# Zero-padding the 64-row key tail to 128 rows and transposing the query tail as whole 128x128 blocks in a fused attention and expert kernel

## The chip, the cores and the metric

The program runs on one core of one Trainium2 chip. The metric is the device time of one execution in microseconds (us); lower is better. A kernel's time is the median of its runs.

## The reference, cut to what matters

Three layers follow each other: a linear attention, a dense layer with an ELU, and four weighted experts. The change touches the attention alone, which works on `q`, `k`, `v` of shape (4 batches, 8 heads, 576 positions, 64):

```python
def phi(x):
    proj = np.einsum('bhsd,df->bhsf', x, w_phi)          # 64 -> 128 features
    proj = proj - np.max(np.abs(proj), axis=-1, keepdims=True)
    return np.concatenate([np.exp(proj), np.exp(-proj)], axis=-1)
q_p, k_p = phi(q), phi(k)
kv  = np.einsum('bhsf,bhsd->bhfd', k_p, v)
z   = np.sum(k_p, axis=2)
num = np.einsum('bhsf,bhfd->bhsd', q_p, kv)
den = np.einsum('bhsf,bhf->bhs', q_p, z)[..., None] + 1e-06
return num / den
```

The result, as 2304 rows of 512, goes through `elu(x @ w_in) @ w_out` with 2048 hidden features and then through four experts with 1024 hidden features each.

## The kernel before, in words

**The attention** goes by pairs of heads: `pair(i)` (L169 to L335) is a generator for one pair, and there are 16 pairs. A sequence of 576 positions is four blocks of 128 and a tail of 64. The host has laid out the last 64 positions of k and of q side by side, so that one matmul (L215) projects both tails at once into a tile whose rows 0 to 63 are the key tail and rows 64 to 127 the query tail; `guard` (L199 to L203) subtracts the row maximum and leaves it in `md`.

From there the two halves go different ways. The key half is exponentiated with both signs into `kpm` (L224, by `kexp`, L205 to L207), a tile of 64 rows. For each of two heads h and two signs c, `kv(h, c)` (L234 to L237) sums k_p^T v in PSUM: four matmuls of 128 rows from `kp` (L236), then one of 64 rows from `kpm` (L237), with `v` in a tile `vt` whose unset columns hold 1.0 so that z comes out beside kv. A float32 matmul is two instructions, so one pair has 32 of L236 and 8 of L237, and "one tail" below means one such L237 matmul of two instructions; there are 4 tails in a pair and 64 in all. The query blocks are transposed on the matmul engine (`tpose`, L239 to L244; the instruction is on L243, four 128x128 blocks in one call), and the query tail by two transposes of rows 64 to 127 (L281), each giving 64 columns. `qexp` (L252 to L262) exponentiates the transposed blocks out of PSUM.

Pairs 0 to 6 (`wide`, i < `NF32`) hold their operands as float32; the other nine split them into a high and a low float32r part on ScalarE and GpSimd (L181, L182, L261, L266).

**The order of the work.** The program is written out in Python, as generators that are advanced in turn: `attention()` starts a new pair every `ATT_LAG` = 5 steps; `weight_stream()` loads the 64-bit weights of the dense layer and converts each piece in steps (`convert64`, L100 to L121: loads on SP at L102, ScalarE at L108, L114, L119, VectorE at L110 to L113, GpSimd at L116, L118, L121) through `CVB` = 3 buffers into a ring of 16 weight tiles. The main loop (L744 on) mixes them with units of the dense layer (`Elu`, matmuls at L524 to L526 and L553 to L555), which goes through all 2304 rows twice, for the first and the second half of the hidden features. The weights of the second half go into the ring as the first half's last row tiles release it. A scheduler that places instructions by its own estimate of their times then fixes the order on each engine. After the attention come the rest of the dense layer and the expert stage, which the change does not touch.

**What sets up the tiles.** `ident`, the two `vt` tiles and `wbl` are made on GpSimd at the start (L157 to L164, of which the `vt` memsets on L160). `kpm` is allocated anew for each pair, from one buffer.

Of the kernel before, what the change touches and what calls it, by code (L numbers as in the profile page):

```python
# [8 lines left out]
F32 = mybir.dt.float32  # L9
# [8 lines left out]
B, H, S, D, FEAT = 4, 8, 576, 64, 128  # L18
NT, DM, DFF, E, F2 = 2304, 512, 2048, 4, 1024
P = 128  # L20
# [42 lines left out]
def attn_elu_moe_kernel(ctx: ExitStack, tc: tile.TileContext, kq_in, vv, w_phi, w_in, w_out, probs, w1, w2, out):  # L63
    nc = tc.nc
    V, A, G, PE, SP = nc.vector, nc.scalar, nc.gpsimd, nc.tensor, nc.sync
# [5 lines left out]
    def pool(name, bufs=1, stack=ctx, **kw):  # L71
        return stack.enter_context(tc.tile_pool(name=name, bufs=bufs, reuse_waits="tile", **kw))
# [53 lines left out]
    a1 = pool("a1", stack=att)  # L126
    wbd = a1.tile([P, 2, FEAT], F32, name="wbd")
    ident = a1.tile([P, P], F32, name="ident")
# [4 lines left out]
    def load(i):  # L133
        b, p = divmod(i, NP)
        kq = ld.tile([P, 2 * S], F32, tag="kq", name="kq")
        SP.dma_start(kq[:, :640], kq_in[b, p, :, :640])
        if i == 0:
            SP.dma_start(wbd, w_phi)
        SP.dma_start(kq[:, 640:], kq_in[b, p, :, 640:])
        v = vt[i % 2]  # L140
        SP.dma_start(v[:, 0:4, 0:D], vv[b, p, :, 0:4, :])
        SP.dma_start(v[:, 4:8, D:P], vv[b, p, :, 4:8, :])
        SP.dma_start(v[0:D, 8, 0:D], vv[b, p, 0:D, 8, :])
        SP.dma_start(v[0:D, 9, D:P], vv[b, p, D:P, 8, :])
        return kq, v

    def bank(shape=(P, 512)):
        return psum.tile(list(shape), F32, tag="bank", name="bank")
# [9 lines left out]
    for i in range(2):  # L158
        t = a1.tile([P, 10, P], F32, name=f"vt{i}")
        G.memset(t, 1.0)  # L160
        vt.append(t)
    loaded = {0: load(0)}
    A.activation(wbh, wbd, ACTF.Copy)
    G.tensor_tensor(out=wbl, in0=wbd, in1=f32(wbh), op=ALU.subtract)  # L164

    def blocks(t, n):
        return t[:, :n * P].rearrange("p (n f) -> p n f", f=P)

    def pair(i):  # L169
        b, p = divmod(i, NP)  # L170
        kq, v = loaded.pop(i)
# [33 lines left out]
        def kexp(d0, d1, src):  # L205
            A.activation(d0, src, ACTF.Exp)
            A.activation(d1, src, ACTF.Exp, scale=-1.0)  # L207

        kp = [a1.tile([P, 4, 2, P], F32, tag=f"kp{j}", name=f"kp{j}") for j in range(2)]
        kpm = a1.tile([D, 2, 2, P], F32, tag="kpm", name="kpm")  # L210
        md = a1.tile([P, 2, P], F32, tag="md", name="md")
        qd = [a1.tile([P, 4, P], F32, tag=f"qd{j}", name=f"qd{j}") for j in range(2)]
        kh = halves(kt)
# [7 lines left out]
        guard(kp[1][:, :, 1], proj(kh, 1), 4)  # L221
        qh = halves(qt)
        yield
        kexp(kpm[:, :, 0], kpm[:, :, 1], md[:D])  # L224
        kexp(kp[1][:, :, 0], kp[1][:, :, 1], kp[1][:, :, 1])
        guard(qd[0], proj(qh, 0), 4)
        if i + 1 < B * NP:
# [4 lines left out]
        pk = bank((P, 4, P))  # L232

        def kv(h, c):  # L234
            for t in range(4):
                PE.matmul(pk[:, 2 * h + c], kp[t // 2][:, t % 2 * 2 + h, c], v[:, 4 * h + t], start=(t == 0), stop=False)  # L236
            PE.matmul(pk[:, 2 * h + c], kpm[:, h, c], v[:D, 8 + h], start=False, stop=True)  # L237

        def tpose(j):  # L239
            pt = bank()  # L240
# [9 lines left out]
            el = a1.tile([P, 2, 2, S], F32R, tag="el", name="el")  # L250

        def qexp(ps, c0, n):  # L252
            src = ps[:, :2 * n].rearrange("p (h s) -> p h s", h=2)
            if wide:
                for c, sc in ((0, 1.0), (1, -1.0)):
                    A.activation(ew[:, :, c, c0:c0 + n], src, ACTF.Exp, scale=sc)
                return None
            ef = a1.tile([P, 2, 2, n], F32, tag=f"ef{n}", name="ef")
            for dst in (ef, eh[:, :, :, c0:c0 + n]):
                for c, sc in ((0, 1.0), (1, -1.0)):  # L260
                    A.activation(dst[:, :, c], src, ACTF.Exp, scale=sc)  # L261
            return ef  # L262
# [7 lines left out]
        else:  # L270
            kvh = a1.tile([P, 4, P], F32R, tag="kvh", name="kvh")
            kvl = a1.tile([P, 4, P], F32R, tag="kvl", name="kvl")
        ef0 = qexp(tpose(0), 0, 256)
        kv(0, 0)
        kv(0, 1)
        yield
        split(ef0, 0, 256)
        ef1 = qexp(tpose(1), 256, 256)
        pt = bank()
        for h in range(2):  # L280
            PE.transpose(pt[:, h * D:(h + 1) * D], md[D:P, h], ident[D:P, D:P])  # L281
        efm = qexp(pt, 512, D)
        kv(1, 0)
        kv(1, 1)
        A.activation(kvw if wide else kvh, pk, ACTF.Copy)
# [53 lines left out]
    def attention():  # L339
        live = []  # L340
        nxt = 0
        step = 0
        while nxt < B * NP or live:
            if nxt < B * NP and step % ATT_LAG == 0:
                live.append(pair(nxt))
                nxt += 1
            for g in list(live):
                if next(g, True):
                    live.remove(g)
                    done[0] += 1  # L350
                else:
                    yield
            step += 1
# [528 lines left out]
```

## Time and profile before

| what | value |
|---|---|
| runs | 1439.26 us median of 3 (1438.32 to 1442.92) |
| the profiled execution's own time | 1437.72 us |
| its span, first to last instruction | 1435.9 us |
| TensorE (PE) busy, matmuls | 1406.3 us, 98% of the span |
| VectorE (DVE), ScalarE (ACT), GpSimd (POOL) busy | 703.2, 621.7, 446.3 us |
| chain of work that ended last | PE 81%, DVE 9%, DMA 4%, issue 2%, ACT 2%, POOL 2% |

In the table and the rows below, PE is the engine's matmuls and PEld its weight loads, which overlap them. L237 is line 237 of the kernel. A busy share of PE says little by itself, because matmuls are pipelined and the profile models their ends; the chain says better how far apart they come. In the chain, the length of a piece is how far it moves the end of the work on. An engine's idle time is followed in brackets by what ended it.

### The profile page before, as it was taken

The page shows a single profiled execution, that of the slowest core. Times are in us where ns is not written, and L with a number is a line of the kernel's source. Part 1 is how long each engine was busy: PE and PEld are TensorE (multiplying, and loading weights), DVE is VectorE, ACT ScalarE, POOL GpSimd, SP SyncE. Part 2 cuts the span into 40 slices and gives each one's busy share as a digit, 9 for nine tenths or more (in the row PEclk, how much of TensorE's full clock was granted, in tenths as well). Part 3 has the DMA queues.
Part 4 walks back from the last instruction along what each step waited for, and adds up shares of the span by engine and source line. Part 5 has one row for each costly group of instructions (what it writes and reads, how often), then busy time and mean ns, then how long its engine had stood idle before and what let it go on. Part 6 is the DMA issues. An engine that isn't in the chain of part 4 may idle for free.

```text
span 1435.9 us, 22308 instructions
## 1 busy us (share of the span) xinstructions
PE 1406.3 (98%) x8688; PEld 1295.8 (90%) x8688; DVE 703.2 (49%) x1150; ACT 621.7 (43%) x1348; POOL 446.3 (31%) x498
## 2 busy tenths in 40 slices
PE   7999999999999999999999999999999999999998
PEld 6788999999998999999989989898888989899897
DVE  7999746556489735333434333233432335233332
ACT  6777666576566544334333443122332214222121
POOL 4567654443388712115111341001330004300000
PEclk9999999999999999999999999999999999999999
DMA  4433222111233335313243323524144352433421
GB/s 149 132 117 113 95 66 65 46 56 46 89 97 124 119 118 214 109 43 118 91 152 121 118 67 121 208 89 166 47 147 154 101 204 69 139 110 132 159 83 66
DMA packets 93625, 160.22 MB, mean 112 GB/s; under 512 B 28496, under 2 KB 39888, under 8 KB 93520
## 3 DMA queue, kind: packets, MB, share of 16 engines
q1 hardware_dynamic: 93520, 158.80, 33.4%
q8 instruction: 68, 1.11, 0.3%
q14 instruction: 37, 0.30, 0.1%
HBM read 109.22 MB, written 49.55 MB: 111 GB/s over the span
## 4 chain that ended last, share of the span: by engine, by line
PE 81%; DVE 9%; DMA 4%; issue 2%; ACT 2%; POOL 2%; SPq 0%; DVEq 0%; POOLq 0%; ACTq 0%
PE bank L700 9%; PE bank L701 8%; PE bank L702 8%; PE bank L641 8%; PE bank L643 8%; PE bank L642 8%; PE bank L236 4%; PE bank L524 4%; PE bank L526 3%; PE bank L554 3%; PE bank L553 3%; PE bank L525 3%; PE bank L555 3%; PE bank L315 3%; DVE top L112 2%
## 5 line engine op out<-in xcount | busy, mean ns | idle before, releaser
L700 PE MATMUL bank<-w,h 128*128 128x512 f32 x576 | 224.6, 392 | 3.9 <-ACT h L652 3.9
L641 PE MATMUL bank<-xv,w 128*128 128x384 f32 x672 | 224.2, 339 | 2.4 <-ACT cm L647 2.4
L642 PE MATMUL bank<-xv,w 128*128 128x384 f32 x672 | 226.6, 337 | 0.0
L701 PE MATMUL bank<-w,h 128*128 128x512 f32 x576 | 225.5, 392 | 0.0
L643 PE MATMUL bank<-xv,w 128*128 128x384 f32 x672 | 223.7, 338 | 0.0
L702 PE MATMUL bank<-w,h 128*128 128x512 f32 x576 | 198.3, 391 | 0.7 <-DVE h L653 0.7
L461 POOL TENSOR_TENSOR w<-wst,w 128x256 fp32r<-128x256 f32 x80 | 62.6, 800 | 341.3 <-ACT w L460 337.2
L554 PE MATMUL bank<-gl,w 128*128 128x256 f32 x576 | 162.1, 286 | 4.1 <-DVE gl L537 4.0
L555 PE MATMUL bank<-gh,w 128*128 128x256 f32 x576 | 160.1, 283 | 0.0
L553 PE MATMUL bank<-gh,w 128*128 128x256 f32 x576 | 155.8, 287 | 2.4 <-ACT gh L536 2.3
L641 PEld LDWEIGHTS bank<-xv,w 128*128 128x128 f32 x672 | 126.6, 188 | 10.3 <-ACT cm L647 3.3
L653 DVE SCALAR_TENSOR_TENSOR h<-bank,h 128x384 fp32r<-128x384 f32 x144 | 77.3, 554 | 115.5 <-ACT h L652 115.5
L652 ACT ACTIVATE h<-bank 128x384 fp32r<-128x384 f32 x144 | 66.8, 490 | 151.3 <-PE bank L643 92.0
L700 PEld LDWEIGHTS bank<-w,h 128*128 128x128 f32 x576 | 108.6, 188 | 25.0 <-ACT h L652 5.3
L642 PEld LDWEIGHTS bank<-xv,w 128*128 128x128 f32 x672 | 126.8, 189 | 4.4
L701 PEld LDWEIGHTS bank<-w,h 128*128 128x128 f32 x576 | 108.6, 189 | 20.6
L643 PEld LDWEIGHTS bank<-xv,w 128*128 128x128 f32 x672 | 126.3, 188 | 0.0
L702 PEld LDWEIGHTS bank<-w,h 128*128 128x128 f32 x576 | 107.3, 188 | 20.0 <-DVE h L653 1.6
L554 PEld LDWEIGHTS bank<-gl,w 128*128 128x128 f32 x576 | 110.1, 191 | 6.7 <-DVE gl L537 5.9
L553 PEld LDWEIGHTS bank<-gh,w 128*128 128x128 f32 x576 | 106.0, 191 | 5.3 <-ACT gh L536 4.4
L555 PEld LDWEIGHTS bank<-gh,w 128*128 128x128 f32 x576 | 110.0, 191 | 0.3
L647 ACT ACTIVATE cmab<-bank 128x384 f32<-128x384 f32 x48 | 23.6, 492 | 178.5 <-PE bank L643 178.5
(118 smaller groups left out, 3005.2 us busy)
## 6 DMA issues: line engine op xcount, KB each, us to landing
xv<-xvd SPq DMA_DIRECT2D x42, 768.0 KB, 4.4
wst<-in_w SPq DMA_DIRECT2D x64, 256.0 KB, 2.8
xvd<-xv SPq DMA_DIRECT2D x21, 768.0 KB, 4.4
yscr<-y SPq DMA_DIRECT2D x54, 256.0 KB, 2.1
y<-yscr SPq DMA_DIRECT2D x54, 256.0 KB, 2.9
w<-in_w_in SPq DMA_DIRECT2D x32, 256.0 KB, 2.8
w<-in_w_out SPq DMA_DIRECT2D x32, 256.0 KB, 2.7
kq<-in_kq SPq DMA_DIRECT2D x16, 320.0 KB, 3.0
```

Source lines behind the costliest of these rows:

```text
L461: on[WL[v % len(WL)]].tensor_tensor(out=lo, in0=x, in1=f32(hi), op=ALU.subtract)
L553: PE.matmul(o, w[:, 0, c], self.gh[:, j], start=start, stop=False)
L554: PE.matmul(o, w[:, 0, c], self.gl[:, j], start=False, stop=False)
L555: PE.matmul(o, w[:, 1, c], self.gh[:, j], start=False, stop=stop)
L641: PE.matmul(o, hi[:, c], x[:, 0, kc], start=not more and kc == 0, stop=False, skip_group_check=more)
L642: PE.matmul(o, hi[:, c], x[:, 1, kc], start=False, stop=False, skip_group_check=more)
L643: PE.matmul(o, lo[:, c], x[:, 0, kc], start=False, stop=kc == 1, skip_group_check=more)
L652: A.activation(h[:, 0], c, ACTF.Relu)
L653: V.scalar_tensor_tensor(out=h[:, 1], in0=c, scalar=0.0, in1=f32(h[:, 0]), op0=ALU.max, op1=ALU.subtract)
L700: PE.matmul(self.acc, h[:, 0, c], w[:, 0], start=f == 0, stop=False)
L701: PE.matmul(self.acc, h[:, 0, c], w[:, 1], start=False, stop=False)
L702: PE.matmul(self.acc, h[:, 1, c], w[:, 0], start=False, stop=f == 2 * NQ - 1)
```

## The change

`kpm` becomes one tile of 128 rows for all pairs, allocated once and set to zero on GpSimd before the first load. The exponentials write its rows 0 to 63 as before; rows 64 to 127 stay zero. The tail matmul reads all 128 rows of `kpm` and of `vt` (whose rows 64 to 127 hold 1.0 there, and count as zero in the product). The query tail's transposes take both 128x128 blocks of `md` whole, against the whole identity, and `qexp` reads columns 64 to 127 of each transposed block.

```diff
@@ set-up, after vt
+    kpm = a1.tile([P, 2, 2, P], F32, name="kpm")
+    G.memset(kpm, 0.0)
@@ pair(i)
-        kpm = a1.tile([D, 2, 2, P], F32, tag="kpm", name="kpm")
@@
-        kexp(kpm[:, :, 0], kpm[:, :, 1], md[:D])
+        kexp(kpm[:D, :, 0], kpm[:D, :, 1], md[:D])
@@ kv(h, c)
-            PE.matmul(pk[:, 2 * h + c], kpm[:, h, c], v[:D, 8 + h], start=False, stop=True)
+            PE.matmul(pk[:, 2 * h + c], kpm[:, h, c], v[:, 8 + h], start=False, stop=True)
@@ qexp(ps, c0, n)
-            src = ps[:, :2 * n].rearrange("p (h s) -> p h s", h=2)
+            src = ps[:, :512].rearrange("p (h s) -> p h s", h=2)[:, :, :n] if n > P else blocks(ps, 2)[:, :, P - n:]
@@ the query tail
-            PE.transpose(pt[:, h * D:(h + 1) * D], md[D:P, h], ident[D:P, D:P])
+            PE.transpose(pt[:, h * P:(h + 1) * P], md[:, h], ident)
```

## Rows read from the trace of the kernel before

**Rows 1.** Span and granted TensorE clock of the core.

```profile
core 0: 1435.9 us, clock 0.997
```

**Rows 2.** Busy us of each engine (instructions) by stretch; then granted clock, DMA share, GB/s.

```profile
20.00:100.00 80.00, 77.68 (x446) 64.72 (x445) 75.43 (x143) 60.65 (x155) 47.80 (x67) 1.00 0.40 121
100.00:140.00 40.00, 39.80 (x269) 35.30 (x268) 37.46 (x69) 26.91 (x65) 28.56 (x38) 1.00 0.39 120
140.00:365.00 225.00, 225.00 (x1738) 212.84 (x1738) 134.37 (x194) 145.74 (x329) 111.23 (x120) 1.00 0.19 60
...
400.00:480.00 80.00, 73.92 (x574) 69.75 (x574) 73.32 (x130) 51.39 (x120) 65.96 (x82) 1.00 0.31 103
```

**Rows 3.** The chain's shares by line in 140 to 365 us.

```profile
by line: PE bank L236 16.5%; PE bank L315 13.0%; PE bank L553 8.0%; PE bank L555 7.9%; PE bank L554 7.9%; PE bank L524 7.8%; PE bank L526 7.4%; PE bank L525 7.2%; PE bank L237 6.6%; PE bank L194 4.1%; PE bank L196 3.8%; PE bank L195 3.7%; P
```

**Rows 4.** The chain's shares by line in 20 to 100 us, then in 400 to 480 us.

```profile
by line: DVE rc L324 11.3%; PE bank L236 8.8%; DVE top L112 6.8%; DVE mx L202 6.2%; DMA w<-in_w_out 5.7%; PE bank L315 4.9%; DVE xf L327 4.0%; issue 3.9%; PE bank L237 3.6%; DVE kp L203 3.0%; ACT kp L206 2.9%; DVE qd L203 2.8%; ACT kp L207 
...
by line: DVE top L112 21.7%; DVE top L111 13.0%; issue 10.7%; DVE top L110 10.4%; DVE gl L537 9.4%; DVE pw L113 9.0%; DVE g L535 8.4%; DMA wst<-in_w 3.9%; DMA w<-in_w_in 3.6%; POOL low L116 3.2%; POOL w L121 2.7%; POOL top L118 2.5%; ACT gh
```

**Rows 5.** Single lines: xcount, ns min/median/max, first and last start; rows*columns of the array.

```profile
L236 PE MATMUL bank<-vt,kp x512: 270/275/377, 14.1 to 359.9; 128*128 128x128 f32 x171
...
L237 PE MATMUL bank<-vt,kpm x128: 272/322/373, 15.1 to 360.3; 64*128 64x128 f32 x128
...
L281 PE MATMUL bank<-ident,md x32: 221/247/275, 19.5 to 359.5; 64*128 64x64 f32 x32
```

**Rows 6.** Pieces of the chain around one pair's tails: start us, length us, what.

```profile
329.15 0.44 PE bank L243 x4
329.58 0.89 PE bank L236 x8
330.48 0.41 PE bank L237 x2
330.89 1.09 PE bank L236 x8
331.98 0.42 PE bank L237 x2
332.40 0.32 PE bank L555
332.94 0.12 PE bank L555
...
335.35 0.27 PE bank L281 x2
335.62 1.09 PE bank L236 x8
```

**Rows 7.** L237 alone by stretch: length, PE busy us (instructions), PEld busy (instructions), clock, DMA.

```profile
0.00:20.00 20.00, 1.46 (x6) 0.88 (x6) 1.00 0.61 183
20.00:100.00 80.00, 8.25 (x34) 5.00 (x34) 1.00 0.40 121
100.00:140.00 40.00, 3.88 (x16) 2.35 (x16) 1.00 0.39 120
140.00:365.00 225.00, 17.47 (x72) 10.59 (x72) 1.00 0.19 60
```

**Rows 8.** Timeline of POOL at the start: start us, us, what [idle before].

```profile
0.87 2.27 POOL L160 MEMSET vt<- 128x1280 f32 x2
...
12.56 0.78 POOL L116 TENSOR_TENSOR low<-low,pw 128x256 f32<-128x256 f32 x1 [7.34 <-DVE pw L113]
```

**Rows 9.** Timeline of ACT near 388 us: the first conversions of the second half's weights.

```profile
388.57 0.72 ACT L119 ACTIVATE w<-top 128x256 fp32r<-128x256 f32 x2 [0.40 <-PE bank L526]
```

**Rows 10.** Pieces of the chain near 65 us: where the scheduler put L215.

```profile
64.91 0.42 PE bank L236 x2
65.32 0.43 PE bank L215 x2
65.76 0.67 PE bank L236 x6
```

**Rows 11.** A piece of the chain in the early stretch.

```profile
22.52 4.53 DMA w<-in_w_out
```

## The prediction

> **What bounds the kernel now.** First the core's span and clock [rows 1]: the clock is at its full level almost throughout, so no time is to be won or lost there. Then the busy time by stretch [rows 2], because the change lies wholly before 365 us and the question is what ends last there. From 140 to 365 us PE is busy for all of 225 us while VectorE works for 134 and no other engine for over 146. From 20 to 100 us PE (77.7 of 80) and VectorE (75.4) are both nearly full, and so from 100 to 140 us. From 400 to 480 us VectorE is again near its end (73.3 of 80).
>
> A busy PE may be waiting inside, so the chain decides. In 140 to 365 us all its large shares are PE's own lines [rows 3]: what makes PE's instruction stream shorter there makes the kernel shorter. In 20 to 100 us the two largest groups on VectorE's side, the reciprocal L324 and the conversion L112, alternate with PE and ACT, and L237 has a small share; in 400 to 480 us the chain is VectorE's conversions [rows 4]. So a gain on PE should arrive nearly whole in the long stretch and only in part in the early one.
>
> **What a tail costs now.** The edited matmul and transposes are the only three forms to compare [rows 5]: L236 uses 128 rows of the array, L237 and L281 use 64, and 128 L237 instructions make 64 tails. The page's durations are modelled, so I price them by how far they move the chain [rows 6]. Eight L236 after 128-row work take 0.89 us, 0.111 each. The two L237 of a tail take 0.41 where two L236 would take 0.22: 0.19 more. The eight L236 behind the tail take 1.09 instead of 0.89: 0.20 more. That second part is not peculiar to L236, for L555 behind another tail takes 0.32 where its next takes 0.12. A tail thus costs 0.39 us over two 128-row instructions in its place. For the query tail, the two L281 take 0.27 where two of the four L243 (0.44 for four, 0.11 each) take 0.22, and the eight L236 behind take 1.09, not 0.89: 0.05 + 0.20 = 0.25 us for each pair.
>
> **What the change makes of it.** A padded tail has the form of L236, and whole-block transposes have the form of L243. Bounds for the new tail's instruction are 0.111 us (L236) and 0.205 us (L237 as it stands); I take 0.111, since shape, type and operand memory are then those of L236. For the transposes the bounds are 0.11 (L243) and 0.135 (L281 now); I take 0.11. Saved on PE: 64 x 0.39 = 25.0 us and 16 x 0.25 = 4.0 us, 29.0 us in all, or 0.45 us for each tail with its quarter of a pair of transposes.
>
> By stretch [rows 7], two instructions a tail: 3 tails before 20 us, 17 in 20 to 100, 8 in 100 to 140, 36 in 140 to 365. At 0.45 each that is 1.4, 7.7, 3.6 and 16.2 us of PE time.
>
> How much of each arrives:
> - 140 to 365 us: PE is the chain, so nearly all. Waits of a few tenths may come up between PE and ACT or GpSimd, whose slack is 79 and 114 us of 225. Bounds 12 and 16.2; I take 16.0.
> - 100 to 140 us: the chain can shorten by at most VectorE's idle time, 40 - 37.46 = 2.5 us, if VectorE's work stays put. Bounds 0.5 and 3.6 (where VectorE's backlog is worked off later, behind PE's); I take 2.0.
> - 20 to 100 us: VectorE's idle time is 80 - 75.43 = 4.6 us; the PE gain is 7.7. Bounds 0.5 and 7.7; with two nearly full engines in turn on the chain I take about half of VectorE's room, 2.5.
> - Before 20 us there are many waits besides; bounds 0 and 1.4; I take 0.5.
>
> Sum: 16.0 + 2.0 + 2.5 + 0.5 = 21.0 us.
>
> **What else is added or moved.** The memset of 512 columns goes to GpSimd once. Two memsets of 1280 columns took 2.27 us [rows 8], so 512 cost some 0.45 us, an estimate from that row; bounds 0.1 and 1.1. GpSimd has 7.34 us idle before its first conversion step in the same rows, which hides it; only `wbl` is queued behind it, and the narrow pairs need that first, over 100 us later. Without the cover the price would be those 0.45 us once. The first tail gains a wait for that memset, which ends near 3.6 us, while the first tail starts at 15.1 [rows 5]; behind it on PE would be the whole stream, but it is over by 11 us. The exponentials write as many elements as before and `qexp` reads as many; its 64-column runs now lie 128 apart, which I put at nothing, between -1 and +1 us over 16 pairs since PE and not ACT ends the stretch. The next pair's exponentials wait for this pair's tails as before, since `kpm` had one buffer. No DMA is added or moved, and no queue passed.
>
> **Does the gain last beyond 365 us?** The VectorE-bound stretch from 400 us would swallow it if its work were waiting for something else than PE. But the first piece of the second half's weights, L119, was released by PE's L526 [rows 9]: the ring slot comes free when the first half's last matmul on it ends. The stretch should begin earlier by what PE gained, unchanged in length, and all that follows with it.
>
> The profiled execution took 1437.72 us, 1.8 over its span; less 21.0 that is 1416.7. The median of the runs shown is 1.5 us higher, so the forecast against it is **1418 us**.
>
> **A rule that speaks against it.** In the rows a 64-row instruction is dearer than a 128-row one of equal columns [rows 5, 6]. The Trainium skill, page "TensorE: Matmul & The Clock Gate", section "LDWEIGHTS (loading the stationary operand)", says that a weight load takes its time from the number of columns and that the count of rows doesn't matter, and its closing table says that one matmul of 32 rows takes the same time as one of 128. By that rule padding buys nothing on the tail, the first rival below; the trace disagrees with it by 0.39 us a tail.
>
> **The rivals.**
> 1. *The surcharge isn't that of 64 rows.* L237 also closes the sum in PSUM, and reads its own tile; if one of these costs the 0.39 us, the padded tail keeps it. Against it: L281 closes no sum and the work behind it pays the same 0.20 us. What is left then is at most the transposes' 4.0 us on PE, 9 of 16 pairs in the long stretch: 0 to 3 us, so about 1437 us. Chance 0.07.
> 2. *All of it arrives.* VectorE only filled its time because it waited its turn among PE's results, and works its conversions off later, where it has 91 us of room: 29 us, 1410 us. Against it stand VectorE's 94% in 20 to 140 us. Chance 0.08.
> 3. *Freed time turns into waits.* The narrow pairs' splits on ACT and GpSimd come late for a faster PE, in the long stretch too, and a third to two thirds of the 21 us are lost: 5 to 13 us, about 1430 us. Against it: in that stretch neither engine is busy for two thirds of the time. Chance 0.10.
> 4. *Slower: conversions slip.* The scheduler places work by its own times, and it does mix pairs: L215 of the next pair stands inside one kv sum [rows 10]. With other tails and transposes it may put VectorE's conversion steps behind the reciprocals in the early stretch, so that a weight buffer is refilled late. One such refill on the chain cost 4.53 us [rows 11]. It takes five of them to eat 21 us; six give 27 - 21 = +6, about 1445 us. Nothing in the profile asks for that many. Chance 0.07, of which 0.01 ends within the bound of no change.
>
> **How the numbers follow.** The forecast, a gain of 13 to 25 us, has 0.68. A measurement can tell some 0.3% from no change, 4.3 us: the forecast and rivals 2 and 3 are faster (0.68 + 0.08 + 0.10 = 0.86), rival 1 and the mild end of rival 4 are the same (0.08), the rest of rival 4 slower (0.06). The range takes the forecast's 1414 to 1426, most of rival 2 down to 1411 and the near part of rival 3 up to 1428; beyond lie the rest of rivals 2 and 3 and all of 1 and 4.
>
> **What would show it.** L237 and L281 stand in the new trace as 128*128 forms; two tail instructions take 0.22 us of the chain, and eight L236 behind a tail 0.89 again. The attention's last L236 starts near 339 us instead of 359.9; the stretch in which VectorE is full stays as long and begins some 21 us sooner; VectorE's share in 20 to 100 us goes above 94%. Wrong would be: pieces of 0.41 us at 128 rows (rival 1); PE waits for ACT or POOL in the long stretch (3); a weight load on the early chain several times over, with PE idle behind it (4).

## The result, and the profile after

The changed kernel takes **1423.53 us** (median of 4 runs, 1422.43 to 1424.97) against 1438.79 us for the kernel before in the same comparison (median of 4, 1437.66 to 1442.92). The ratio is 0.9889, 95% interval 0.9867 to 0.9911: 15.3 us, or 1.1%, faster. The profiled execution took 1424.05 us with a span of 1422.3 us. The forecast was 1418 us within 1411 to 1428, so the time lies inside the range, 5.5 us on the slow side.

First the price, the part that a reader can check piece by piece against [rows 6]. The changed lines in the new trace (L237 is the old L236, L238 the old L237, L244 the old L243, L282 the old L281), forms first and then the chain around one pair (start us, length us):

```profile
L238 PE MATMUL bank<-vt,kpm x128: 273/275/275, 15.0 to 344.1; 128*128 128x128 f32 x128
```

```profile
321.36 0.44 PE bank L244 x4
321.80 0.22 PE bank L282 x2
322.01 0.89 PE bank L237 x8
322.91 0.22 PE bank L238 x2
323.13 0.89 PE bank L237 x8
324.03 0.22 PE bank L238 x2
324.25 0.12 PE bank L196
```

Two tail instructions take 0.22 us instead of 0.41, the eight instructions behind them 0.89 instead of 1.09, two transposes 0.22 instead of 0.27, with 0.89 behind them. The prices came out as written, to the last digit that the view shows.

Next, the stretches, to hold against [rows 2] (busy us of PE, PEld, DVE, ACT and POOL with counts; then clock, DMA share, GB/s):

```profile
20.00:100.00 80.00, 70.05 (x437) 61.31 (x436) 77.23 (x146) 60.33 (x155) 49.11 (x69) 1.00 0.41 124
100.00:140.00 40.00, 39.03 (x291) 36.72 (x292) 33.45 (x71) 27.29 (x68) 28.62 (x39) 1.00 0.40 125
140.00:342.00 202.00, 200.32 (x1657) 198.51 (x1656) 132.38 (x186) 139.43 (x312) 102.43 (x110) 1.00 0.21 65
...
400.00:480.00 80.00, 73.41 (x572) 69.39 (x571) 69.26 (x120) 50.84 (x118) 65.54 (x79) 1.00 0.34 111
```

From 20 to 100 us PE has fallen from 77.7 to 70.1 busy us, while VectorE has gone up to 77.2 of 80. PE's new idle time there is a wait for VectorE: the transposes L244 (the old L243) wait for the query blocks that VectorE makes (engine, line, what it waited for: us in all, times, longest; before, then after):

```profile
PE bank L243 <- DVE qd L203: 1.8, 2, 1.3
...
PE bank L244 <- DVE qd L205: 6.9, 5, 2.0
```

and in the chain of that stretch, which PE shared before [rows 4], VectorE's lines now lead (those shown add up to 65%, before to 34%):

```profile
by line: DVE rc L325 15.2%; DVE mx L204 12.1%; DVE top L112 7.5%; DVE xf L328 7.1%; issue 6.8%; DVE top L110 6.6%; DVE qd L205 5.2%; DVE kp L205 4.0%; DVE top L111 3.7%; DMA w<-in_w_in 3.4%; DVE pw L113 3.2%; PE bank L194 3.2%; PE bank L316
```

Where the gain arises and where it is given back can be read off milestones: the start of the last tail instruction of a pair, of the first second-half weight (L119, its 33rd), and of the first matmul of the expert stage (us from the span's start, from the two traces). A milestone compares like with like only where PE has started as many matmul instructions before it in both, so their number stands beside it:

| milestone | before | after | gain | instructions before it |
|---|---|---|---|---|
| last tail of pair 0 | 21.09 | 19.56 | 1.5 | 69, 69 |
| last tail of pair 4 | 84.22 | 82.90 | 1.3 | 408, 408 |
| last tail of pair 6 | 138.91 | 135.79 | 3.1 | 765, 765 |
| last tail of pair 8 | 188.48 | 186.95 | 1.5 | 1139, 1157 |
| last tail of pair 9 | 212.07 | 206.62 | 5.5 | 1321, 1321 |
| last tail of pair 15 | 360.30 | 344.13 | 16.2 | 2471, 2471 |
| first second-half weight written | 388.57 | 374.86 | 13.7 | 2704, 2726 |
| first matmul of the expert stage | 665.05 | 650.65 | 14.4 | 4896, 4896 |
| span | 1435.9 | 1422.3 | 13.6 | 8688, 8688 |

Pair 8's 1.5 is not a loss of that size, because in the changed kernel the scheduler has put 18 more matmuls of the dense layer ahead of that tail, some 2.2 us at 0.12 us each (PE's count in the first bracket; before, then after, up to just short of the tail):

```profile
0.00:188.47 188.47, 178.53 (x1139) 155.53 (x1140) 158.28 (x293) 131.34 (x318) 118.62 (x156) 1.00 0.38 118
0.00:186.94 186.94, 166.89 (x1157) 153.04 (x1158) 156.34 (x293) 131.95 (x321) 118.45 (x157) 1.00 0.39 120
```

Some 29 us of PE time were removed, 1.81 a pair; 16.2 are left when the attention's last tail starts. From pair 9 to pair 15 the gain grows by 10.7, all but 0.2 of what these six pairs free. Pairs 7 to 9 bring 2.3 of 5.4, and pairs 0 to 6 bring 3.1 of 12.7. Then 2.5 are lost again before the second half's weights start. The experiments ask why. (The two profiled executions lie 13.7 us apart, the medians 15.3; runs of one kernel differ by up to 5 us here, so the milestones account for the traces and not for the last 2 us.)

### The profile page after: what moved, and what is told of

It reads as the page before. It is cut to its first block, busy times and chain, and to the rows that moved or that the text cites. A ratio compares the mean times of both kernels' runs of the same rounds, so it can differ in the third digit from the quotient of the medians.

```text
span 1422.3 us, 22325 instructions
## 1 busy us (share of the span) xinstructions
PE 1380.5 (97%) x8688; PEld 1286.9 (90%) x8688; DVE 698.2 (49%) x1150; ACT 619.9 (44%) x1348; POOL 446.7 (31%) x499
## 4 chain that ended last, share of the span: by engine, by line
PE 74%; DVE 11%; DMA 5%; POOL 4%; issue 3%; ACT 3%; SPq 0%; DVEq 0%; POOLq 0%; ACTq 0%
PE bank L701 8%; PE bank L702 8%; PE bank L703 8%; PE bank L642 8%; PE bank L643 7%; PE bank L644 7%; PE bank L555 3%; PE bank L556 3%; PE bank L554 3%; PE bank L527 3%; PE bank L525 3%; PE bank L526 3%; PE bank L237 2%; PE bank L316 2%; DMA wst<-in_w 2%
## 5 line engine op out<-in xcount | busy, mean ns | idle before, releaser
L556 PE MATMUL bank<-gh,w 128*128 128x256 f32 x576 | 160.9, 284 | 0.0
L703 PEld LDWEIGHTS bank<-w,h 128*128 128x128 f32 x576 | 107.3, 188 | 20.0 <-DVE h L654 1.6
L556 PEld LDWEIGHTS bank<-gh,w 128*128 128x128 f32 x576 | 110.1, 191 | 0.2
```

The costliest lines, as they stand in the source:

```text
L556: PE.matmul(o, w[:, 1, c], self.gh[:, j], start=False, stop=stop)
L703: PE.matmul(self.acc, h[:, 1, c], w[:, 0], start=False, stop=f == 2 * NQ - 1)
```

## The experiments

The theory: a 64-row instruction among 128-row ones costs PE the surcharge of [rows 6]; PE sets the end behind 140 us, and VectorE does before. The rivals: that the surcharge belongs to something else than the 64 rows; and that part of the gain is lost in every pair alike. Each set of runs had its own runs of the kernel before (medians of 1439.5 to 1441.0 us), so the ratios are compared, not the medians.

**1. The two edits apart.** Padded tails alone (e1), whole transposes alone (e2):

```diff
  e1: the changed kernel, with
-            PE.transpose(pt[:, h * P:(h + 1) * P], md[:, h], ident)
+            PE.transpose(pt[:, h * D:(h + 1) * D], md[D:P, h], ident[D:P, D:P])
  (and qexp's source as before);  e2: the kernel before, with the reverse
```

> Only the key tail is padded; the query tail's transposes stay at 64 rows. Theory (each 64-row tail costs 0.39 us of PE more than a 128-row one, each pair's transposes 0.25): tail pieces of 0.22 us and 0.89 us behind them, L282 still 0.27 and 1.09; 25 of the 29 us of PE go, so 25/29 of the whole change's 15 us arrive: 12 to 14 us below the kernel before. Rival (the whole-block transposes bring most of it): under 5 us.

> Only the query tail's transposes are whole blocks; the key tail stays at 64 rows. Theory: L281 takes 0.22 us for two and the eight matmuls behind it 0.89; 4 of 29 us of PE go, 2.2 of them after 140 us: 1.5 to 3 us below the kernel before. Rival (64-column transposes cost no more than others in the stream): within 1 us of the kernel before.

The tails alone: 1425.15 us, ratio 0.9895 (0.9881 to 0.9910), as much as the whole change within the intervals. The transposes alone: 1440.27 us, 0.9999 (0.9988 to 1.0010): nothing, where 1.5 to 3 us were expected, a miss. In e2's trace pair 15's last tail starts 1.0 us sooner than before (359.26), but the first second-half weight 1.9 us later (390.43). What lies between shows in the number of matmul instructions that PE has started up to that weight, x in the first bracket (stretch from 0 to the start of L119's 33rd; the kernel before, the changed one, e1, e2):

```profile
0.00:388.57 388.57, 378.63 (x2704) 346.68 (x2705) 269.87 (x448) 255.58 (x589) 202.13 (x244) 1.00 0.29 89
```

```profile
0.00:374.86 374.86, 354.81 (x2726) 340.54 (x2727) 269.39 (x449) 255.66 (x591) 204.30 (x246) 1.00 0.30 93
```

```profile
0.00:374.08 374.08, 356.51 (x2704) 339.51 (x2705) 266.28 (x448) 253.58 (x590) 202.68 (x245) 1.00 0.30 92
```

```profile
0.00:390.43 390.43, 380.42 (x2728) 351.55 (x2729) 268.01 (x448) 256.31 (x591) 203.95 (x245) 1.00 0.29 89
```

In the changed kernel and in e2 the scheduler puts 22 and 24 more matmuls of the dense layer ahead of the one that frees the first ring slot; at 0.12 us each [rows 6] that is 2.6 to 2.9 us. e1 keeps the old count and loses nothing there (14.3 us at pair 15, 14.5 at the weight). So the transposes do save PE time up to pair 15; what was missed is the order that follows.

**2. The early and the late pairs apart.** The whole change for pairs 7 to 15 alone (e3), for pairs 0 to 6 alone (e4):

```diff
+            rows = P if not wide else D        # e4: P if wide else D
+            PE.matmul(pk[:, 2 * h + c], kpm[:rows, h, c], v[:rows, 8 + h], start=False, stop=True)
  (the transposes and qexp's source by the same condition)
```

> The change for the nine later pairs alone (7 to 15), whose tails lie behind 140 us. Theory (what is saved before 140 us is hidden by a full VectorE): nearly the whole gain is here, 12 to 15 us below the kernel before. Rival (a share of each pair's saving is lost wherever it lies): 9/16 of 15.3, some 8.6 us.

> The change for the seven early pairs alone (0 to 6). Theory: VectorE is full there, so 12.5 us of PE bring 0 to 4 us in all. Rival (a share of each pair's saving is lost wherever it lies): 7/16 of 15.3, some 6.7 us.

Late pairs: 1426.76 us, ratio 0.9905 (0.9891 to 0.9919), 13.7 us of 1438.8. Early pairs: 1438.53 us, ratio 0.9986 (0.9976 to 0.9996), 2.0 us of 1438.8. Nine pairs bring nearly all and seven nearly nothing, though each pair frees the same 1.8 us of PE: the rival with an equal share per pair (8.6 and 6.7) is out. The early pairs are also the `wide` ones, and no run takes place and kind of pair apart; that it is the place is read from PE's waits for VectorE in the early stretch, not shown by these two runs.

Their traces also say where pairs 7 to 9 of the changed kernel fell short. In e4, where those pairs have nothing to gain, the early pairs are 2.5 us ahead at pair 6's last tail and only 0.4 at pair 9's and at pair 15's. In e3 the nine late pairs are 14.1 us ahead at pair 15, of 16.3 freed. From these two traces the loss looks to be mostly the early pairs' gain, given back behind 138 us, where PE had no idle time before and now waits (changed kernel, 136 to 160 us; e4 has two waits of the same length there, e3 has only 0.1 us):

```profile
PE bank L555 <- POOL gl L538: 1.2, 2, 1.1
PE bank L244 <- DVE qd L205: 0.6, 1, 0.6
```

**3. Is it the 64 rows?** The tail put first in its sum, so that a 128-row matmul closes it (e5), and the tail over 96 rows (e6):

```diff
  e5: the kernel before, with
+            PE.matmul(pk[:, 2 * h + c], kpm[:, h, c], v[:D, 8 + h], start=True, stop=False)
             for t in range(4):
                 PE.matmul(..., start=False, stop=(t == 3))
  e6: the changed kernel, with
+            PE.matmul(pk[:, 2 * h + c], kpm[:96, h, c], v[:96, 8 + h], start=False, stop=True)
```

> The kernel before with each sum's 64-row tail put first (it opens the sum in PSUM) and a 128-row matmul closing it. Theory (the surcharge is that of 64 rows among 128): the two L237 instructions still take some 0.41 us of the chain and the 128-row work behind them 0.20 more, the time stays within 3 us of the kernel before. Rival (closing the sum costs it): the tail takes 0.22 us and the surcharge moves to the last L238 of each sum.

> The changed kernel with the tail matmul over 96 rows of kpm and vt instead of 128 (32 rows of zeros, transposes whole). Theory (rows up to 64 are set up as half an array, 96 as the whole): start to start 0.11 us as with 128 rows, time within 2 us of the changed kernel. Rival (any count under 128 pays): 0.39 us a tail come back, and the time is within 3 us of the kernel before.

e5, one run: 1441.91 us beside 1441.04 for the kernel before. Its chain (the tail is L235, the 128-row matmuls L237):

```profile
340.41 0.41 PE bank L235 x2
340.83 1.09 PE bank L237 x8
```

The surcharge stays with the 64-row instruction and what follows it; closing the sum has no part in it. e6, one run: 1424.93 us, within 2 us of the changed kernel, and in its chain

```profile
318.17 0.22 PE bank L238 x2
318.39 0.89 PE bank L237 x8
```

96 rows cost what 128 do. So the tile need not be full: 96 rows are on the side of 128, where 64 are not. Counts between 64 and 96 were not tried.

**4. Is it the change of rows, or each 64-row instruction?** The two 64-row tails of a head one behind the other (e12), PSUM's sums opened once for the bank:

```diff
  the kernel before, in kv(h, c):
-            PE.matmul(pk[:, 2 * h + c], kpm[:, h, c], v[:D, 8 + h], start=False, stop=True)
+            for k in range(2 * c):
+                PE.matmul(pk[:, 2 * h + k], kpm[:, h, k], v[:D, 8 + h], start=False, stop=True, ...)
```

> The kernel before with 64-row tails, but the two tails of a head issued one after the other behind their eight 128-row matmuls, so that the array changes between 128 and 64 rows half as often. Theory A (the surcharge belongs to the change of rows alone): four L238 take some 0.52 us of the chain (0.205 and three of 0.11), 0.20 behind them; half the surcharge goes, 12 us of PE, and 5 to 8 us of time. Theory B (each 64-row instruction that follows another on the same half of the array pays as well): four L238 take some 0.84 us, 0.20 behind; 0.18 us saved for each two tails, 6 us of PE, and 2 to 4 us of time. Padding to 128 rows stays ahead of both.

1430.98 us, ratio 0.9930 (0.9916 to 0.9945): 8 to 12 us, more than either theory gave. The chain:

```profile
322.70 0.44 PE bank L244 x4
323.13 1.79 PE bank L236 x16
324.92 0.64 PE bank L238 x4
325.56 0.32 PE bank L556
325.88 0.11 PE bank L554
```

Four 64-row instructions take 0.64 us, 0.41 + 0.23: the second two cost no more than 128-row ones. Behind them stands the same 0.20 as before (L556 at 0.32 instead of 0.12). Theory A holds: the surcharge belongs to the change of rows, 0.19 us on the way in and 0.20 on the way out, with two or with four tail instructions between. The expected 0.52 was wrong in one point: it counted one slow start on the way in, and there are two. In e12's trace the starts around these four lie 0.205 and 0.213 us apart on the way in, then 0.112 and 0.111, then 0.202 and 0.223 on the way out; L236's 128-row instructions otherwise start 0.112 apart, the dense layer's 0.12. Why 8 to 12 us arrive of the 12 that PE saves, where the whole change brings 15 of 29, no run shows. The Trainium skill's page "TensorEngine Tiling (Array Packing)", section "Key Properties", says that a change of tiling mode drains TensorE; this trace agrees with a price for each change and gives it: 0.39 us for going to 64 rows and back, alike for two and for four tail instructions. The query tail's transposes, which have 64 columns, cost 0.25 [rows 6].

**5. What VectorE hides.** Both kernels without the reciprocals:

```diff
-            V.reciprocal(out=rc[:, s], in_=rc[:, s])
```

> The kernel before without the 32 reciprocals (62 us of VectorE, 27 of them before 140 us; the output is multiplied by the denominator instead of divided). Theory (VectorE is full before 140 us and PE nearly as full): a little faster than the kernel before, 3 to 9 us, since PE's own stall before 140 us is some 9 us. Rival (VectorE doesn't matter there): within 2 us of the kernel before.

> The changed kernel without the 32 reciprocals, as in e7. Theory (the early pairs' 12.5 us of PE were hidden by VectorE): with VectorE relieved they arrive, and this kernel is 22 to 28 us below e7, against the 15 us between the changed kernel and the one before. Rival (they are lost to the order of work or to waits for ACT and GpSimd): 13 to 17 us below e7.

e7: 1443.62 us, ratio 1.0024 (1.0012 to 1.0037), 2 to 5 us slower where 3 to 9 us faster were expected, a miss; e8: 1424.09 us, ratio 0.9883 (0.9864 to 0.9902). Between them lie 19.5 us, more than the change's 15.3 but short of the theory's 22. The experiment didn't relieve VectorE where it was meant to (stretch 20 to 100 us, e7 and then e8):

```profile
20.00:100.00 80.00, 79.38 (x463) 66.92 (x462) 75.05 (x155) 64.55 (x168) 57.64 (x80) 1.00 0.44 134
```

```profile
20.00:100.00 80.00, 72.54 (x445) 63.62 (x444) 75.66 (x154) 64.68 (x169) 59.49 (x82) 0.98 0.45 134
```

VectorE is as full as before, because the scheduler drew conversions forward into the room (the 17th L119 runs at 70 us in both, at 90 and 88 in the full kernels). Pair 4's last tail again gains nothing (85.2 and 86.6 us). Behind it the gain grows faster, to 20.0 us at pair 15. Part of the larger gain has another reason: e7, like e8, has 2726 matmul instructions before the first second-half weight, so the 2.5 us that the change loses there against the kernel before are not lost against e7. So these two runs don't show that VectorE hides the early pairs' saving; for that there are PE's waits for VectorE and what e4 measured.

**6. Three tries to beat the changed kernel.** A conversion step moved off VectorE (e9), whole transposes for early pairs only (e10), and the dense layer's first two row tiles taken together (e11):

```diff
  e9
-        V.tensor_scalar(out=f32(top), in0=f32(top), scalar1=MINF, scalar2=MAXF, op0=ALU.max, op1=ALU.min)
+        G.tensor_scalar(out=f32(top), in0=f32(top), scalar1=MINF, scalar2=MAXF, op0=ALU.max, op1=ALU.min)
  e10: e1, with whole-block transposes if wide
  e11
-    for t, u in order(TAIL, 0):
+    for t, u in sorted(order(TAIL, 0), key=lambda tu: (tu[1], tu[0]) if tu[0] < 2 else (HU, 0)):
```

> The changed kernel with one of the four VectorE steps of each weight conversion, the clamp on L110, moved to GpSimd (64 x 0.29 us off VectorE, half of them before 145 us). Theory (VectorE hides the early pairs' saving): the early pairs come sooner, 2 to 6 us below the changed kernel. Rival (the conversion's chain gets longer by a hop, and GpSimd is slow at it): 0 to 6 us above the changed kernel.

> The key tail padded for all pairs, whole-block transposes for the seven early pairs alone. In the traces so far every kernel with whole-block transposes in the later pairs issues 2726 to 2728 matmuls before the first second-half weight is written (L119), the others 2704. Theory (those 22 matmuls, 2.6 us, are what the transposes' 2.2 us in the later pairs are given back for): 2704 again, and within 2 us of the changed kernel, of the padded tails alone too. Rival (the whole transposes' saving in the later pairs arrives in the end): 2 to 3 us above the changed kernel.

> The changed kernel with the dense layer's first two row tiles taken together, weight pair by weight pair, so that PE gets twice the work for each converted weight while VectorE is full. Theory (before 140 us PE waits for VectorE, whose conversions are due too early): PE's idle time there is filled and the freed 12 us of PE come out in part, 3 to 9 us below the changed kernel. Rival (the four accumulator banks that two open row tiles hold leave the attention too few): 0 to 10 us above the changed kernel.

e9: 1448.21 us, ratio 1.0055 (1.0039 to 1.0072), 25 us above the changed kernel, a miss beyond the rival's bound. The clamp takes far longer on GpSimd (changed kernel, then e9; ns min/median/max):

```profile
L110 DVE TENSOR_SCALAR top<-top x64: 222/290/850, 8.6 to 460.2; 128x256 f32<-128x256 f32 x64
```

```profile
L110 POOL TENSOR_SCALAR top<-top x64: 1052/1064/1520, 8.5 to 498.1; 128x256 f32<-128x256 f32 x64
```

and the stretch from 100 to 140 us of e9 reads

```profile
100.00:140.00 40.00, 29.00 (x160) 25.20 (x160) 31.17 (x47) 22.58 (x57) 36.95 (x46) 0.79 0.30 94
```

Pairs 0 to 2 come up to 1.2 us later, but pairs 3 to 5 come 1.2 to 3.7 us sooner (pair 5's last tail starts at 107.3 us instead of 111.0, with five matmul instructions fewer ahead of it), which speaks for VectorE as their bound; then the conversions are late, GpSimd is the full engine (36.95 of 40) and PE stands idle for 11 of 40 us. The granted clock is 0.79 in the mean of that stretch: PE was busy for 0.74 of the 5.6 us before 115.6 us, and from there to 132.4 us the clock stood at 0.50, its lower level of 1.2 GHz:

```profile
110.00:115.60 5.60, 0.74 (x4) 0.54 (x4) 4.67 (x7) 5.06 (x15) 4.84 (x7) 1.00 0.21 64
115.60:132.40 16.80, 10.85 (x35) 8.77 (x36) 11.81 (x17) 6.05 (x16) 15.73 (x19) 0.50 0.24 72
```

e10: 1423.91 us, ratio 0.9890 (0.9874 to 0.9906), the changed kernel's time. It reaches pair 15's last tail 2.4 us later than the changed kernel (346.51) and the first second-half weight 0.3 us sooner (374.60), with 2704 matmuls before it: what the late whole transposes save, the altered order gives back. But whole transposes are not needed for such an order: e7, whose transposes are those of the kernel before, has 2726 too, which the expectation above overlooked.

e11: 1434.44 us, ratio 0.9964 (0.9951 to 0.9977), 11 us above the changed kernel, a miss. PE idles for 6 of 60 us from 140 to 200 us, waiting for VectorE, ACT and GpSimd in turn. That the accumulators leave too few banks was argued, not shown. No try beats the changed kernel.

## Why the prediction was right, and where it was not

**The bound by stretch** was right. Late pairs bring 13.7 us and early ones 2.0 (e3, e4), as the chain's shares by stretch had it [rows 3, 4].

**The price of a tail and of the transposes** was right: 0.39 and 0.25 us in [rows 6], gone in the new trace. Rival 1 is out: the padded tail still closes its sum and reads its own tile, and costs 0.22; and e5 moved the closing away without moving the surcharge. But the rule that the prediction held against the change was misread. The Trainium skill's page "TensorE: Matmul & The Clock Gate", section "LDWEIGHTS (loading the stationary operand)", says that the time of a weight load goes by the columns and not by the count of rows; on that this trace agrees to within 8 ns (kernel before; ns min/median/max):

```profile
L236 PEld LDWEIGHTS bank<-vt,kp x512: 186/192/192, 14.0 to 359.8; 128*128 128x128 f32 x171
L237 PEld LDWEIGHTS bank<-vt,kpm x128: 182/184/186, 15.1 to 360.2; 64*128 64x128 f32 x128
```

Inside a group of 64-row matmuls the matmuls are no dearer either (e12, 0.11 us for each of the later two). The time went into the change from one count to the other, of which that section says nothing.

**The sum, 21.0 us, was too high by 5.7** by the medians, and by the milestones of the two traces it failed in these terms. The time lies inside the range because the range left room for 10 us of such losses.
- *20 to 100 us, taken at 2.5 us.* The gain goes from 1.5 (pair 0) to 1.3 (pair 4): nothing. Half of VectorE's idle time was expected to go; some of it did (75.4 to 77.2 busy of 80), but the pairs came no sooner. Here, with VectorE full to 94% and on the chain, PE's freed 7.7 us were worth nothing by pair 4.
- *100 to 140 us, 2.0 us, and before 20 us, 0.5 us.* 1.8 (pair 4 to pair 6) and 1.5 came.
- *140 to 365 us, taken at 16.0 us.* 13.1 came between pairs 6 and 15. From pair 9 on the rule "PE is the chain" holds almost to the tenth (10.7 of 10.9). The shortfall lies in pairs 7 to 9, with 1.8 us of new PE idle time between 138 and 154 us, 1.2 for GpSimd and 0.6 for VectorE; VectorE is busy for 22.7 of the 24 us from 136 to 160 us, so its full stretch reaches some way beyond the 140 us at which the forecast drew the line. The other 1.3 us of the shortfall stay open.
- *"The stretch should begin earlier by what PE gained."* It began 13.7 us sooner and not 16.2. The row read for it [rows 9] was right in that PE's matmul frees the slot; it was overlooked that the scheduler may put other matmuls ahead of that one. With whole transposes in the late pairs it did so (e2 and the changed kernel against e1 and e10); that other edits can do it too shows in e7.

**Rival 4, the slip of the order,** was right as a mechanism, but in another place and at a smaller price: not VectorE's conversions in the early stretch at 4.5 us a time, but PE's own order before the second half's weights, 2.5 us once. Of rival 3's waits for ACT and GpSimd one of 1.1 us on GpSimd came up behind 140 us. (Its price is off in itself: when a third to two thirds of 21 us are lost, 7 to 14 are left, not 5 to 13.) Rival 2 is out: VectorE did not give its room back. Of the signs named, the last L236 (now L237) starts at 343.9 us, not near 339; VectorE's share from 20 to 100 us rises to 97%, as forecast.

**The rest at nothing** was right: the memset of `kpm` took 0.52 us, with GpSimd idle behind it (start us, us, what, idle before).

```profile
3.08 0.52 POOL L163 MEMSET kpm<- 128x512 f32 x1
...
12.58 0.78 POOL L116 TENSOR_TENSOR low<-low,pw 128x256 f32<-128x256 f32 x1 [7.42 <-DVE pw L113]
```

## What to carry to other kernels

In this kernel a lone matmul of 64 rows in a stream of 128-row ones cost 0.39 us more than a padded one, half of it in the pieces behind it, where its own duration doesn't show it. So try padding it with zeros, or, where that isn't possible, putting such matmuls together, since the price was paid for each change and not for each instruction (e12). Other types and shapes were not tried. Before counting the gain, split it by the stretches in which the engine sets the end; seven of sixteen pairs here were worth 2 us of 15. And where a scheduler orders the work, take a few us off the sum for an order that comes out differently, and look for it at the points where one matmul releases a buffer.

## What the runs showed of the hardware that was not expected

The change of rows delays two starts on each side, 0.39 us in all, and it costs the same whether two or four tail instructions stand between (e12); 96 rows count as 128 (e6). And 64-row instructions on opposite halves of the array can run side by side: once in the kernel before, the scheduler put a tail (rows 0 to 63) between the query tail's transposes (rows 64 to 127), and the first two start together (timeline of PE: start us, modelled us):

```profile
186.75 0.27 PE L281 MATMUL bank<-ident,md 64*128 64x64 f32 x1
186.76 0.37 PE L237 MATMUL bank<-vt,kpm 64*128 64x128 f32 x1
186.87 0.22 PE L281 MATMUL bank<-ident,md 64*128 64x64 f32 x1
186.97 0.27 PE L237 MATMUL bank<-vt,kpm 64*128 64x128 f32 x1
```

The first two start 0.01 us apart, the others some 0.11 apart, and the next matmul starts 0.42 us after the first, about as long as a tail alone takes. Whether all tails and transposes, paired like that, would beat the padding wasn't tried.
